# Transposing q and k by DMA instead of on TensorE, with the first batch's token stages put back whole

## The chip, the cores and the metric

The kernel runs on one core of a Trainium2 chip. The metric is device time in microseconds (us), the median of several runs. The engines are named as the profile names them: PE (TensorE, matrix products), PEld (its weight loads, which overlap PE), DVE (VectorE), ACT (ScalarE), POOL (GpSimd, which issues the loads), SP (SyncE, which issues the stores). Each engine works through its own queue in order.

## What is computed

Sliding-window attention with a position bias, followed by a token-and-channel mixer. The inputs are float32; the kernel works in bf16 and its output is float32.

```python
# q, k, v: (B, H, S, D) = (8, 8, 576, 64); window 128; slopes 2 ** -(h + 1)
scores = q @ k.T / sqrt(D) - slope_h * |i - j|     # only where 0 <= i - j < 128
attn   = softmax(scores) @ v
x = attn.transpose(0, 2, 1, 3).reshape(8, 576, 512)
h = relu(x^T @ w_tok1) @ w_tok2                    # over tokens: 576 -> 256 -> 576
u = x + h^T
out = u + relu(u @ w_ch1) @ w_ch2                  # over channels: 512 -> 1536 -> 512
```

## The kernel before, in words

**Groups.** Two heads of a batch make a group g; there are four groups per batch (NHP), 32 in all. For each group the kernel does:

- T (`att_T`, line 195): q and k of the group, tokens in the partitions, are transposed so that the head dimension is in the partitions. For the load, tokens are laid out as 96 partitions (RP) of six consecutive tokens (TPP) each, so a group needs 6 transposes of 96x128 for q and 6 for k. They go to one PSUM buffer; ACT copies q's half to `qT`, DVE copies k's half to `kT`, both putting the tokens in order. The argument `early` uses two smaller PSUM buffers and gives both copies to ACT.
- S, E, M (`att_S`, `att_E`, `att_M`), in two halves: scores on PE, exponential with bias on ACT, product with a mask on DVE.
- V (`att_V`, line 263): the weighted sum of v on PE, then a reciprocal and a product on DVE, which write `xb`. With `early` it works head by head.

**Loads.** `dma_qk(b, ...)` on POOL brings q and k of a batch, turned to bf16, into `qn` and `kn` (two each, by parity of the batch). `regroup` on DVE copies them to `qg` and `kg` (two each too), with the slices in the order that T reads. `dma_v` brings v into `vp`.

**Mixer.** For each batch: `tok1` (two, each five matmuls), `tok2` (five), `trans_u` (four, transposes of u), `ch1` (24, each four matmuls, whose relu on ACT writes R2), and the second channel product `ch2_items` (four or five chunks of 512 columns, each in three parts of four matmuls, then an add on DVE and a store on SP). The chunks of a batch run in the mixer of the next batch.

**Order.** The order in every queue is the order of the program text. `spread` (line 17) interleaves a mixer's items with attention work of the batches ahead: main items and side items have weights, and a side item is emitted when its share of the side weight is reached by the main items' share. In the mixer of batch b the side work is `att_step` for four groups, which transposes groups two ahead, scores one ahead, and does V of the current one. In the mixer of batch b the transposes are so those of batch b+1's last two groups and of batch b+2's first two. The regroup for batch b+3 stands at channel tiles 4 and 7 of 12 in mixer b (line 491).

**The start.** Lines 506 to 628 are written out by hand. Batch 0's groups are worked on as the loads arrive. Its token stages run in pairs of heads (`tok1_pair`, `tok2_pair`, with `trans_u` between them), mixed into the attention of batch 0, so that the channel products of batch 0 begin at once after. Half of these run alone (line 604), then all attention of batch 1 is spread over the other half and the first six items of batch 1's mixer (line 614). Then batch 2 is regrouped and the rest of mixer 1 runs with groups 8 and on beside it.

**PSUM.** `ps_at` has two buffers of two banks each, shared in turn by T, S and V (and `tok2_pair`); `ps_ma` has four of one bank, shared by all of the mixer.

Of the kernel before, what the change touches and what calls it, by code (L numbers as in the profile page):

```python
# [38 lines left out]
def kernel(  # L39
# [38 lines left out]
    pepool = ctx.enter_context(tc.tile_pool(name="pe", bufs=3))  # L78
# [12 lines left out]
    qg = [const.tile([P, TPP, H, D], bf16, name=f"qg{i}") for i in range(2)]  # L91
    kg = [const.tile([P, TPP, H, D], bf16, name=f"kg{i}") for i in range(2)]
    vp = [const.tile([P, H, NCH, D + 1], bf16, name=f"vp{i}") for i in range(2)]
    NR = 4
# [26 lines left out]
    def dma_v_tail(b):  # L121
        nc.gpsimd.dma_start(
            out=vp[b % 2][P - TAIL : P, :, NF, 0:D],
            in_=v[b, :, NF * P : S, :].rearrange("h s d -> s h d"),
        )

    def dma_v(b, c):
        nc.gpsimd.dma_start(  # L128
            out=vp[b % 2][:, :, c, 0:D],
            in_=v[b, :, c * P : (c + 1) * P, :].rearrange("h s d -> s h d"),  # L130
        )

    def dma_v_head(b, h):
        nc.gpsimd.dma_start(
            out=vp[b % 2][:, h, 0:NF, 0:D],
            in_=v[b, h, 0 : NF * P, :].rearrange("(c p) d -> p c d", p=P),
        )

    def regroup(b, h0, h1, which=(0, 1)):

        for n in which:
            raw, t = ((qn, qg), (kn, kg))[n]
            nc.vector.tensor_copy(  # L143
                out=t[b % 2][:RP, :, h0:h1, :],
                in_=raw[b % 2][:RP, h0:h1, :].rearrange("p h (j d) -> p j h d", j=TPP),
            )
# [48 lines left out]
    def att_T(g, early=False):  # L195
        b, hp = divmod(g, NHP)
        if early:
            tt = [ps_ma.tile([P, 1024], bf16, name="tT1", tag="ma") for _ in range(2)]
        else:
            t2 = ps_at.tile([P, 2, 1024], bf16, name="tT", tag="at")  # L200
            tt = [t2[:, n, :] for n in range(2)]
        for n, t_raw in ((0, qg), (1, kg)):
            for j in range(TPP):
                nc.tensor.transpose(  # L204
                    tt[n][:, j * RP : (j + 1) * RP],
                    t_raw[b % 2][:RP, j, 2 * hp : 2 * hp + 2, :].rearrange("p h d -> p (h d)"),
                    ident[:RP, :RP],
                )
        def nat(n):
            return tt[n][:, 0:S].rearrange("c (j p) -> c p j", j=TPP)  # L210
        def dst(a):
            return a[:, :].rearrange("c (p j) -> c p j", j=TPP)
        nc.scalar.copy(out=dst(qT[g % NR]), in_=nat(0))  # L213
        (nc.scalar.copy if early else nc.vector.tensor_copy)(out=dst(kT[g % NR]), in_=nat(1))  # L214

# [47 lines left out]
    def att_V(g, early=False):  # L263
# [5 lines left out]
        if early:  # L269
            ots = [ps_ma.tile([P, 512], f32, name="ot1", tag="ma") for _ in range(2)]  # L270
        else:
            ot = ps_at.tile([P, 2, 512], f32, name="ot", tag="at")
            ots = [ot[:, i, :] for i in range(2)]
        for i in range(2):
# [7 lines left out]
            for n, (qb, pb, col, kc) in enumerate(mms):  # L282
                nc.tensor.matmul(  # L283
                    ots[i][:, qb * (D + 1) : (qb + 1) * (D + 1)],
                    lhsT=pb[:, i, col : col + P], rhs=vb[:, h, kc, :],
# [3 lines left out]
        xs = xb[b][:, :, 2 * hp * D : (2 * hp + 2) * D].rearrange("p c (i d) -> p i c d", i=2)  # L289
        if early:  # L290
            for i in range(2):
                o3 = ots[i][:, 0 : NCH * (D + 1)].rearrange("p (c e) -> p c e", e=D + 1)
                nc.vector.reciprocal(out=rt[:, i, :, None], in_=o3[:, :, D : D + 1])
                nc.vector.tensor_tensor(  # L294
                    out=xs[:, i, :, :], in0=o3[:, :, 0:D],
                    in1=rt[:, i, :, None].broadcast_to([P, NCH, D]), op=ALU.mult,
                )
        else:
            o4 = ot[:, :, 0 : NCH * (D + 1)].rearrange("p i (c e) -> p i c e", e=D + 1)
            nc.vector.reciprocal(out=rt[:, :, :, None], in_=o4[:, :, :, D : D + 1])  # L300
            nc.vector.tensor_tensor(  # L301
                out=xs, in0=o4[:, :, :, 0:D],
                in1=rt[:, :, :, None].broadcast_to([P, 2, NCH, D]), op=ALU.mult,
            )
# [15 lines left out]
    def att_step(g):  # L320

        its = []
        if g + 2 < NG:
            its.append((0.6, lambda: att_T(g + 2)))
# [22 lines left out]
    def tok2(b, c):  # L347
        if c == 0:
            ubs[b] = upool.tile([P, NCH, DM], bf16, name="ub", tag="ub", bufs=3)
# [8 lines left out]
        )  # L358

    def tok1_pair(hp):  # L360

        t1 = ps_ma.tile([P, NDH, P], f32, name="t1p", tag="ma")
        for dh in range(NDH):
            for c in range(NCH):
                nc.tensor.matmul(
                    t1[:, dh, :], lhsT=W1[:, c, dh * P : (dh + 1) * P],
                    rhs=xb[0][:, c, hp * P : (hp + 1) * P],
                    start=(c == 0), stop=(c == NCH - 1),
                )
        r1t = rpool.tile([P, DM], bf16, name="r1t", tag="r1t", bufs=4)  # L370
        nc.scalar.activation(
            out=r1t[:, 0 : NDH * P], in_=t1[:, :, :].rearrange("p j x -> p (j x)"), func=ACT.Relu
        )
        r1s[hp] = r1t

    def tok2_pair(hp):
        if hp == 0:
# [286 lines left out]
```

## Time and profile before

| | |
|---|---|
| time, median of 3 runs | 328.44 us (328.26 to 331.09) |
| profiled execution, own time | 328.44 us |
| its span | 326.6 us |
| PE busy | 299.9 us (92%) |
| PEld busy | 194.2 us (59%) |
| ACT busy | 180.4 us (55%) |
| DVE busy | 178.6 us (55%) |
| POOL busy | 60.9 us (19%) |
| granted PE clock | 0.999 |
| the software DMA queue's packets (loads) | 55.3% of 16 engines' span |
| the hardware DMA queue's packets (stores) | 8.3% |

The span is the time from the first to the last instruction of one profiled execution. PE's busy time overstates how full PE is, because matmuls are pipelined and their ends are modelled: the distance between the starts of neighbouring matmuls is the better measure. Some groups of instructions that the change touches, with count, busy us and the mean of one:

| line | what | count | busy us | mean ns |
|---|---|---|---|---|
| L204 | PE, transposes of q and k | 384 | | 203 to 281 |
| L213 | ACT, copies to qT from PSUM | 32 | | about 640 |
| L214 | DVE, copies to kT from PSUM | 28 | 21.2 | 757 |
| L143 | DVE, regroup of a whole batch | 14 | 13.6 | 946 to 1070 |
| L245 | ACT, exponentials | 128 | 79.9 | 692 |
| L420 | ACT, relu after ch1 | 192 | 72.8 | 423 |
| L253 | DVE, product with the mask | 64 | 43.7 | 688 |
| L356 | DVE, u add of batches 1 to 7 | 35 | 22.9 | 683 |
| L388 | DVE, u add of batch 0, by pairs | 4 | 3.3 | 819 |

### The profile page before, as it was taken

Reading aid. Unit: us, or ns where it says so; the run is one execution under the profiler, and the core shown is the slowest. Engines: PE = TensorE matmul, PEld = TensorE weight load, DVE = VectorE, ACT = ScalarE, POOL = GpSimd, SP = SyncE. Lnnn points to the kernel's source line nnn. Section 1 sums busy time; section 2 is a strip of 40 time slices with the busy share of each in tenths; the row PEclk is TensorE's granted clock in tenths of the full one; section 3 lists DMA queues with packets and bytes.
Section 4 is the critical chain, followed back from the end, with each engine's and each line's share of the span. In section 5 each row is a group of like instructions: output and inputs, shape, how many; then the busy total and the mean of one; then the engine's idle time right before and its main releaser. Section 6 shows DMA issues by size and latency. Waiting matters only on the chain.

```text
span 326.6 us, 6808 instructions
## 1 busy us (share of the span) xinstructions
PE 299.9 (92%) x2876; PEld 194.2 (59%) x2876; DVE 178.6 (55%) x343; ACT 180.4 (55%) x379; POOL 60.9 (19%) x81
## 2 busy tenths in 40 slices
PE   2797978796999999998999999998999999999995
PEld 1475854443775567655775567755775567647742
DVE  4996246869554875358453775358433762343021
ACT  3973897171995328753795418743785139313800
POOL 8993151622015000410005000310000000000000
PEclk9999999999999999999999999999999999999999
DMA  6999999995879111991009110191001010011022
GB/s 87 157 165 203 200 167 154 217 159 115 134 102 147 37 67 38 157 89 66 34 0 100 39 66 34 11 95 65 35 2 32 34 69 30 2 64 64 2 64 97
DMA packets 59502, 27.76 MB, mean 85 GB/s; under 512 B 38672, under 2 KB 54864, under 8 KB 59472
## 3 DMA queue, kind: packets, MB, share of 16 engines
q0 software_dynamic: 54224, 17.90, 55.3%
q1 hardware_dynamic: 5248, 9.44, 8.3%
q8 instruction: 22, 0.36, 0.5%
q14 instruction: 8, 0.07, 0.1%
HBM read 35.78 MB, written 9.44 MB: 138 GB/s over the span
## 4 chain that ended last, share of the span: by engine, by line
PE 72%; DVE 16%; ACT 7%; DMA 2%; issue 1%; POOL 1%; POOLq 0%
PE ct L415 23%; PE ht L352 4%; PE sp L233 4%; PE tT L204 4%; ACT pe L245 4%; PE ot L283 4%; DVE pb L253 3%; DMA kn_87<-in_k_dram 2%; ACT R_104 L420 2%; DVE xb L301 2%; DVE ub L356 1%; DVE obt L455 1%; DVE xb L294 1%; DVE kT_100 L214 1%; PE ut L402 1%
## 5 line engine op out<-in xcount | busy, mean ns | idle before, releaser
L415 PE MATMUL ct<-UT,WC_107 128*128 128x288 bf16 x768 | 103.5, 286 | 2.7 <-DVE UT L407 1.6
L245 ACT ACTIVATE pe<-sp,biascol 128x512 bf16<-128x512 f32 x128 | 79.9, 692 | 19.4 <-PE sp L233 13.6
L420 ACT ACTIVATE R_104<-ct 128x288 bf16<-128x288 f32 x192 | 72.8, 423 | 32.1 <-PE ct L415 26.5
L415 PEld LDWEIGHTS <-WC_107 128*128 128x128 bf16 x768 | 72.4, 98 | 24.0 <-issue 5.0
L253 DVE TENSOR_TENSOR pb<-pe,masks 128x1024 bf16<-128x1024 bf16 x64 | 43.7, 688 | 50.8 <-ACT pe L245 50.8
L443 PEld LDWEIGHTS <-R_104 128*128 128x128 bf16 x432 | 40.3, 98 | 43.3
L283 PEld LDWEIGHTS <-pb 128*128 128x128 bf16 x576 | 22.9, 100 | 5.2 <-DVE pb L253 0.7
L356 DVE TENSOR_TENSOR ub<-ht,xb 128x512 bf16<-128x512 f32 x35 | 22.9, 683 | 3.8 <-PE ht L352 3.8
L128 POOL DMA_DIRECT2D vp_94<-in_v_dram x16 | 15.0, 945 | 49.6 <-PE ot L283 45.1
L301 DVE TENSOR_TENSOR xb<-ot,rt 128x640 bf16<-128x640 f32 x28 | 23.1, 824 | 1.0
L352 PE MATMUL ht<-r1t,W_106 128*128 128x512 bf16 x70 | 18.9, 379 | 0.0
L128 POOL DMA_DIRECT2D vp_93<-in_v_dram x12 | 10.5, 894 | 43.1 <-PE ot L283 35.4
L213 ACT COPY qT_95<-tT 128x576 bf16<-128x576 bf16 x7 | 4.5, 638 | 21.4 <-PE tT L204 21.2
L213 ACT COPY qT_98<-tT 128x576 bf16<-128x576 bf16 x7 | 4.5, 642 | 21.3 <-PE tT L204 21.3
L300 DVE RECIPROCAL rt<-ot 128x10 f32<-128x10 f32 x28 | 6.0, 215 | 12.2 <-PE ot L283 12.2
L204 PEld LDWEIGHTS <-qg_89 96*128 96x128 bf16 x96 | 6.1, 106 | 9.8 <-DVE qg_89 L143 8.1
L283 PE MATMUL ot<-vp_94,pb 128*128 128x65 bf16 x288 | 11.6, 194 | 0.2 <-DVE xb L301 0.2
L339 PEld LDWEIGHTS <-W_105 128*128 128x128 bf16 x70 | 6.4, 98 | 8.6 <-issue 1.5
L407 DVE COPY UT<-ut 128x576 bf16<-128x576 bf16 x28 | 11.1, 447 | 0.5 <-PE ut L402 0.5
L214 DVE COPY kT_101<-tT 128x576 bf16<-128x576 bf16 x7 | 5.3, 756 | 10.3 <-ACT qT_97 L213 10.3
L402 PE MATMUL ut<-ident,ub 128*128 128x128 bf16 x128 | 10.9, 219 | 0.0
L214 DVE COPY kT_99<-tT 128x576 bf16<-128x576 bf16 x7 | 5.3, 757 | 9.6 <-ACT qT_95 L213 9.6
(217 smaller groups left out, 394.9 us busy)
## 6 DMA issues: line engine op xcount, KB each, us to landing
out_dram<-obt SPq DMA_DIRECT2D x32, 256.0 KB, 2.0
qn_86<-in_q_dram POOLq DMA_DIRECT2D x4, 576.0 KB, 9.7
kn_88<-in_k_dram POOLq DMA_DIRECT2D x4, 576.0 KB, 11.5
vp_94<-in_v_dram POOLq DMA_DIRECT2D x16, 128.0 KB, 6.1
qn_85<-in_q_dram POOLq DMA_DIRECT2D x3, 576.0 KB, 9.3
kn_87<-in_k_dram POOLq DMA_DIRECT2D x3, 576.0 KB, 11.9
WC_107<-in_moe_w_ch_dram POOLq DMA_DIRECT2D x3, 512.0 KB, 9.0
WC_108<-in_moe_w_ch_dram POOLq DMA_DIRECT2D x1, 1536.0 KB, 22.9
```

Of the source, the lines that this page charges most:

```text
L128: nc.gpsimd.dma_start(out=vp[b % 2][:, :, c, 0:D], in_=v[b, :, c * P : (c + 1) * P, :].rearrange("h s d -> s h d"),)
L204: nc.tensor.transpose(tt[n][:, j * RP : (j + 1) * RP], t_raw[b % 2][:RP, j, 2 * hp : 2 * hp + 2, :].rearrange("p h d -> p (h d)"), ident[: ...
L245: nc.scalar.activation(out=pe[:, i, :], in_=sp[:, i, :], func=ACT.Exp, bias=biascol[:, h : h + 1], scale=scale,)
L253: nc.vector.tensor_tensor(out=pb[:, :, :], in0=pes.pop((g, half))[:, :, :], in1=masks[:, half, 2 * hp : 2 * hp + 2, :], op=ALU.mult,)
L283: nc.tensor.matmul(ots[i][:, qb * (D + 1) : (qb + 1) * (D + 1)], lhsT=pb[:, i, col : col + P], rhs=vb[:, h, kc, :], start=(n == 0), stop=( ...
L301: nc.vector.tensor_tensor(out=xs, in0=o4[:, :, :, 0:D], in1=rt[:, :, :, None].broadcast_to([P, 2, NCH, D]), op=ALU.mult,)
L352: nc.tensor.matmul(ht[:, :], lhsT=W2[:, j, c0(c) : c0(c) + P], rhs=r1s[b, j][:, :], start=(j == 0), stop=(j == NDH - 1),)
L356: nc.vector.tensor_tensor(out=ubs[b][:, c, :], in0=ht[:, :], in1=xb[b][:, c, :], op=ALU.add)
L402: nc.tensor.transpose(ut[:, main0 + c * P : main0 + (c + 1) * P], ubs[b][:, c, cb * P : (cb + 1) * P], ident[:, :],)
L415: nc.tensor.matmul(ct[:, :], lhsT=WC1[:, cb, ht_i * P : (ht_i + 1) * P], rhs=UT[:, cb, o : o + SH], start=(cb == 0), stop=(cb == NCB - 1),)
L420: nc.scalar.activation(out=R2[:, ht_i, o : o + SH], in_=ct[:, :], func=ACT.Relu)
L443: nc.tensor.matmul(o2[0][:, :], lhsT=R2[:, ht_i, col : col + P], rhs=WC2[:, ht_i, :], start=(ht_i == 0 and c != NF), stop=(ht_i == NHT - 1),)
```

## The change

For batches 2 to 7, `att_T` makes no PE transposes. Instead a new function, `dma_trans`, issues two DMA transposes per batch on SP: all of `qg` (96 partitions x 3072) into `tq`, all of `kg` into `tk`. The copies to `qT` and `kT` remain, one on ACT and one on DVE, now reading those tiles in SBUF. Batches 0 and 1 are transposed on PE as before. `qg` and `kg` become one tile each; `tq` and `tk` are two each. `dma_trans(b)` is called right after the regroup of batch b: in the mixer, after channel tile 7 of mixer b-3; by hand for batches 2 and 3.

The start is another one: batch 0's token stages are not done in pairs but after its attention, as for the other batches, mixed with regroup, transposes and scores of batch 1's first two groups; its UT copies move from ACT to DVE; the other two groups' scores are spread over the channel products of batch 0, and V of batch 1 over the first six items of mixer 1. After `dma_trans(2)` the next four items of mixer 1 (two `tok1`, two parts of a chunk) run without side work. v's tiles have another order of dimensions; some pools have a buffer less; loads are issued in another order.

```diff
-    pepool = ctx.enter_context(tc.tile_pool(name="pe", bufs=3))
+    pepool = ctx.enter_context(tc.tile_pool(name="pe", bufs=2))
...
-    qg = [const.tile([P, TPP, H, D], bf16, name=f"qg{i}") for i in range(2)]
-    kg = [const.tile([P, TPP, H, D], bf16, name=f"kg{i}") for i in range(2)]
-    vp = [const.tile([P, H, NCH, D + 1], bf16, name=f"vp{i}") for i in range(2)]
-    NR = 4
+    qg = const.tile([P, TPP, H, D], bf16, name="qg")
+    kg = const.tile([P, TPP, H, D], bf16, name="kg")
+    tq = [const.tile([P, TPP * NHP, RP], bf16, name=f"tq{i}") for i in range(2)]
+    tk = [const.tile([P, TPP * NHP, RP], bf16, name=f"tk{i}") for i in range(2)]
+    vp = [const.tile([P, NCH, H, D + 1], bf16, name=f"vp{i}") for i in range(2)]
+    NR = 3
...
+    def dma_trans(b):
+
+        for src, t in ((qg, tq), (kg, tk)):
+            nc.sync.dma_start_transpose(
+                out=t[b % 2][:, :, :], in_=src[:RP, :, :, :].rearrange("p j h d -> p (j h d)")
             )
...
     def att_T(g, early=False):
         b, hp = divmod(g, NHP)
+        if b < 2:
...
+            src = [t[:, 0:S].rearrange("c (j p) -> c p j", j=TPP) for t in tt]
         else:
+            src = [
+                t[b % 2][:, :, :].rearrange("c (j n) p -> c n p j", n=NHP)[:, hp, :, :]
+                for t in (tq, tk)
+            ]
+        dst = [t[g % NR][:, :].rearrange("c (p j) -> c p j", j=TPP) for t in (qT, kT)]
+        nc.scalar.copy(out=dst[0], in_=src[0])
+        (nc.scalar.copy if early else nc.vector.tensor_copy)(out=dst[1], in_=src[1])
...
-            its.append((0.6, lambda: att_T(g + 2)))
+            its.append((0.2, lambda: att_T(g + 2)))
...
-            ubs[b] = upool.tile([P, NCH, DM], bf16, name="ub", tag="ub", bufs=3)
+            ubs[b] = upool.tile([P, NCH, DM], bf16, name="ub", tag="ub", bufs=2)
...
-    def tok1_pair(hp):
...
-    def tok2_pair(hp):
...
-        (nc.vector.tensor_copy if b else nc.scalar.copy)(
-            out=UT[:, cb, o : o + S], in_=ut[:, :]
-        )
+        nc.vector.tensor_copy(out=UT[:, cb, o : o + S], in_=ut[:, :])
...
+                if ht_i == 7 and 0 < b < B - 3:
+                    its.append((0.0, lambda: dma_trans(b + 3)))
...
-        for h in range(4):
+        for h in range(H):
             dma_v_head(0, h)
...
-        for h in range(4, H):
-            dma_v_head(0, h)
+        dma_qk(1, 0, H)
...
         att_T(3, True)
-        att_V(0, True)
         build_masks(3)
...
+        att_SEM(2, 1)
+        att_V(0)
+        att_SEM(3, 0)
+        att_V(1)
+        att_SEM(3, 1)
+        att_V(2)
+        att_V(3)
...
+        order = t1 + [
+            lambda: regroup(1, 0, H), lambda: att_T(g), lambda: att_T(g + 1),
+            t2[0], t2[1], lambda: att_SEM(g, 0), t2[2], t2[3], lambda: att_SEM(g, 1), t2[4],
+            lambda: att_SEM(g + 1, 0), *ut, lambda: att_SEM(g + 1, 1),
+        ]
...
+        spread([(0.48, f) for f in c1], side)
+        spread(its1[:n1], [(0.6, lambda x=x: att_V(g + x)) for x in range(NHP)])
         regroup(2, 0, H)
+        dma_trans(2)
...
+        side.append((0.0, lambda: dma_trans(3)))
...
-        spread(its1[n1:], side)
+        for _, f in its1[n1 : n1 + NDH + 2]:
+            f()
+        spread(its1[n1 + NDH + 2 :], side)
```

## The prediction

> **What bounds the kernel now.** I read the page's busy times first, then the table of busy time by stage, then TensorE's (PE's) timeline in one steady mixer, then the fill, then the DMA issues.
>
> The page says PE is busy 92% of the span, but an average hides two regimes. The table by stage (columns: stretch, its length, busy us and count of PE, PEld, DVE, ACT, POOL, then clock, DMA share, GB/s) separates them:
>
> ```profile
> 0.00:32.20 32.20, 20.88 (x263) 15.30 (x264) 24.09 (x90) 19.62 (x33) 25.39 (x39) 1.00 1.24 152
> 32.20:61.40 29.20, 24.39 (x278) 17.25 (x278) 15.55 (x25) 20.69 (x44) 8.32 (x11) 1.00 1.92 180
> 61.40:98.50 37.10, 32.76 (x359) 22.00 (x359) 24.93 (x39) 24.61 (x52) 8.96 (x11) 1.00 1.11 138
> 98.50:135.70 37.20, 36.91 (x356) 23.52 (x354) 22.22 (x37) 21.39 (x47) 5.63 (x7) 1.00 0.60 86
> ...
> 172.30:210.00 37.70, 37.41 (x361) 23.95 (x359) 21.89 (x37) 21.41 (x46) 4.39 (x6) 1.00 0.36 52
> ```
>
> From 98.5 on PE lacks only 0.3 us of 37; DVE and ACT are busy under 60%. Before 61.4 it idles 16 us: the fill, where DVE, ACT and latencies set the end. In steady state, then, PE time saved is time saved. The PE timeline of the mixer of batch 4 shows the price of one transposed group (start, length, line, operation):
>
> ```profile
> 174.04 0.42 PE L204 MATMUL tT<-ident,qg_90 96*128 96x96 bf16 x6
> 174.30 0.42 PE L204 MATMUL tT<-ident,kg_92 96*128 96x96 bf16 x6
> 174.56 1.03 PE L443 MATMUL o_2632<-WC_108,R_104 128*128 128x512 bf16 x4
> ```
>
> Starts are what counts, since ends are modelled: from 174.04 to 174.56, 12 transposes hold PE for 0.52 us, 43 ns each.
>
> **Part 1: TensorE transposes of batches 2 to 7 go.** 6 batches x 4 groups x 0.52 us = 12.5 us of PE. They lie from 62 us to the end of batch 7's, four per mixer: two in the stretch of second channel products, one among the transposes of u, one in the first channel product. Where PE has no gap all of it is gained. In the last of these stretches ACT could take over: the 16.5 us from 193.0 to 209.5 hold 13.4 us of ACT, and from 202.3 to 209.5 ACT is busy without a gap. I discount half of that one group in five mixers: 5 x 0.26 = 1.3. Gain 11.2; bounds 9.4 (a whole group per mixer lost, and the 0.5 us of one more) and 14 (the second half of the scores also waited 0.2 to 0.3 us at 67.0, 88.4 and 94.9 for the PSUM buffer that a transposed group held, which for these batches is no longer taken).
>
> The Trainium skill speaks against the change here: "VectorE: DVE Perf Modes", section "The three transpose paths", gives 390 ns for a 128x128 transpose on TensorE and 1309 ns by DMA, and its rules prefer TensorE where PSUM will do. The 43 ns pitch disagrees with the first figure; by the second, one DMA here (18 such blocks) would be an estimated 23.6 us if nothing overlapped, which is the second rival below.
>
> **Part 2: the copies stay.** Each group keeps its copy of qT on ACT (638 ns) and kT on DVE (757 ns), now from SBUF with a stride of 768 B instead of 192 B. No row has this read; regroup reads in runs at 96x3072 in 950 ns, faster per element. Between 0.4 and 1.5 us each on engines that are not the bound: taken as unchanged.
>
> **Part 3: DMA transposes arrive.** Twelve, each 96x3072 bf16 = 576 KB, on SP's queue, which carries only outputs (332 ns to issue one). SP's in-order queue now waits for the regroup before it can issue, and outputs stand behind it; three output buffers and 2.6 us or more between outputs cover some microseconds. How long one takes (L) no row shows. From the nearest rows:
>
> ```profile
> out_dram<-obt SPq DMA_DIRECT2D x32, 256.0 KB, 2.0
> qn_86<-in_q_dram POOLq DMA_DIRECT2D x4, 576.0 KB, 9.7
> kn_88<-in_k_dram POOLq DMA_DIRECT2D x4, 576.0 KB, 11.5
> ```
>
> At least 2.0 us (an output on the same queue, less than half the bytes), at most 11.9 (the page's slowest load of the same bytes, software queue, reading float32). I take 4.5 us, the output row scaled by bytes (2.0 x 576/256), since queue and packet path are nearest. By the skill's "DMA: Bandwidth & Descriptors", "Latency and other measured facts" (261 GB/s for DMA transposes) with that page's fixed 2 us, L would be an estimated 4.3 us; no run here shows it yet.
>
> Who waits? For batches 4 to 7 the issue stands at the eighth of twelve channel tiles of a mixer and the first use near the middle of the next mixer, over 20 us later: hidden up to L = 10 in series. For batch 2 it is not. Before, the first tok1 of batch 1 starts at 61.4 and its regroups end at 62.2 and 63.4, that is 0.8 and 2.0 us later. After, the transposes start then. The code runs two tok1 (2.2 us) and two parts (1.7) first, then the spread places one part (0.86) and one tok2 (0.43) before group 8's scores: cover of 5.2 us. Scores are ready at: k transposed, plus kT's copy 0.85. In series: 0.8 + 9.0 + 0.85 = 10.6, a stall of 5.4; side by side: 2.0 + 4.5 + 0.85 = 7.4, a stall of 2.2. I take 4. Ends: L = 2 in series, 4.8 + 0.85, 0.4 us; L = 11.9 side by side 9.6, in series 20. ACT and DVE queue up behind these two copies (relu, ub), so PE cannot run far past them. For batch 3 the scores come about 10 us after the issue: 0, but 4 at L = 11.9 side by side and 15 in series. One qg and one kg also make the next regroup wait until these were read; a mixer later, free.
>
> **Part 4: the fill goes back to whole-batch stages.** Now group 3's xb is stored at 28.1 and the first ct starts at 31.3, since token stages ran pair by pair under the scores. After, masks and exponentials still set the pace up to xb (DVE is 9.2 us busy from 10 to 20); without the four ub adds (3.3 us) but with each product behind its own exponential, I leave it at 28.1. Then DVE's queue must run, before ct: swap 0.6, regroup of batch 1 1.9, two kT 1.5, five ub adds of 0.68, three products of 0.69, four UT copies of 0.45 = 11.3 us. With about 1 us of gaps ct starts at 40.4, 9 us late, but four of eight score halves of batch 1 are done. ACT then has 24 relu x 0.42 + 5 exponential pairs x 1.2 + 2 qT x 0.64 = 17.4 us against 14.4 of PE: about 57.5. Then six parts of 0.86 and four value groups of 0.57 on PE, 7.5 us, and the last xb 0.4: 65.4, where now it is 61.3. Loss 4; bounds 1 (ACT's tail overlaps the parts) and 8 (gaps as the 5 us that this stretch shows now).
>
> **Smaller edits.** Fewer buffers (qT/kT 4 to 3, exponentials 3 to 2, ub 3 to 2): each is reused at least a step after its last reader. The order of vp and the spread weight 0.2 touch no bound: nothing. q and k of batch 1 loaded ahead of the channel weights: those are now issued at 17.1 and land in 11 us or less, and ct comes 9 us later: covered, else 2 us.
>
> **Sum.** The profiled run's own time is 328.44, span 326.6 and 1.84 around it; it is also the median. 328.4 - 11.2 + 4 + 4 = 325.2, rounded to 325.
>
> **Rivals.**
> - *Cover suffices.* Transposes of 2 to 3 us in series: 0.4 to 2 us of stall, fill at its lower half: 328.4 - 12 + 2.5 + 1 = 320. For it: no large DMA elsewhere on SP's queue. Against: value loads of batch 2 and q and k of batch 4 are issued at 60.4 to 66, with the DMA engines 90% busy or more up to 73.
> - *The DMA becomes the wait (slower).* Place: group 8's scores, then batch 3's. It decides when the two stalls exceed 7.2 + 3.3 us: with 2L - 3.55 for batch 2 and 2L - 9.15 for batch 3 in series that is L = 5.8, side by side (L - 2.35 and L - 8.2) L = 10.5. At 11.9 side by side: 328.4 - 11.2 + 4 + 9.6 + 4 = 335; in series, with 20 and 15, 356, and every mixer would begin to wait. For it: the 9.7 to 11.9 us rows. Against: those read float32 from HBM.
> - *The fill costs more, about 8 to 10* with the stall of 4: 329 to 331. For: 5 us of PE gaps in that stretch now.
> - *It does not do what it says:* if the transposes were split in element-sized pieces, the second rival at its far end; part of its chance.
>
> **Numbers.** No-change shows within about 1%, 325.2 to 331.7 (the three runs span 328.3 to 331.1). Forecast 0.42 (its own range 321 to 328; 0.25 faster, 0.17 same), cover suffices 0.20 (faster), DMA wait 0.28 (slower), heavier fill 0.10 (0.04 same, 0.06 slower). Faster 0.45, same 0.21, slower 0.34. The range, 319 to 340, leaves out the DMA wait's far end (0.13) and the best of the second case (0.06).
>
> **What would show it.** Right: L204 x96 instead of x384; mixers from 98.5 on about 2 us shorter each; a wait of ACT's qT or DVE's kT copy on the DMA of tq or tk once, near 70 us; first ct near 40. Wrong: landing times of tq and tk of 9 us or more with waits in every batch; copies from SBUF well over 1 us; ct pitch growing as much as the transposes saved; a gap at the fill outside 1 to 8 us.

## The result, and the profile after

The changed kernel takes 343.85 us (median of 4 runs, 342.79 to 345.94) where the kernel before took 328.35 beside it: ratio 1.0459 with a 95% interval of 1.0384 to 1.0535, so it is slower by 4.6%. Forecast was 325, with a range of 319 to 340. The profiled run's own time is 344.43, its span 342.7. Medians here and below are of all runs, while ratios and intervals leave out the runs that are more than 1.5% above the fastest of the same kernel.

First the table of busy time by stage of the changed kernel, in the columns of the one before. Its stretches are the kernel's own: to just before the first `ct` (which is at 42.1), to the first `tok1` of batch 1 (65.6), to the end of the wait described below (85.3), to the first chunk product of mixer 2 (122.5), and the rest.

| stage ends at | before | after | its length, after less before |
|---|---|---|---|
| first `tok1` of batch 1 | 61.4 | 65.6 | +4.2 |
| first chunk product of mixer 2 | 98.3 | 122.5 | +20.0 |
| end of the span | 326.6 | 342.7 | -8.1 |

The second row is read from PE's timeline, before and then after:

```profile
98.27 0.39 PE L437 MATMUL o_1575<-ident,UT 128*128 128x128 bf16 x4
```

```profile
122.48 0.39 PE L405 MATMUL o_1427<-ident,UT 128*128 128x128 bf16 x4
```

The busy times of the stretches after:

```profile
0.00:41.00 41.00, 24.70 (x234) 15.09 (x235) 30.40 (x92) 21.76 (x35) 27.07 (x41) 0.98 1.23 162
41.00:65.60 24.60, 23.38 (x250) 16.54 (x248) 11.43 (x21) 15.26 (x36) 6.63 (x8) 0.96 2.02 162
65.60:85.30 19.70, 5.34 (x26) 2.26 (x27) 3.45 (x5) 3.41 (x4) 5.55 (x6) 0.71 1.37 174
85.30:122.50 37.20, 30.34 (x259) 18.45 (x260) 21.24 (x37) 24.19 (x47) 3.53 (x5) 0.83 0.65 96
122.50:342.70 220.20, 212.86 (x1768) 130.38 (x1765) 110.23 (x189) 122.69 (x251) 19.03 (x22) 1.00 0.51 78
```

Read the PE column against the length of the stretch. The last stretch is as full as before (212.9 of 220.2 us, before 222.1 of 228.3), and shorter. The loss is in the third and fourth: of 56.9 us PE works in 35.7, and the granted clock is 0.71 and 0.83. The chain of waits between 70 and 86 says which wait ends last (start, length, what):

```profile
70.52 0.70 DVE obt L423
71.23 0.07 SPq L153
71.30 0.05 issue
71.34 13.20 DMA tk_93<-kg
84.55 0.02 issue
84.57 0.66 DVE kT_102 L227
85.23 0.05 issue
85.28 1.03 PE sp L246 x10
```

One DMA, the transpose of k of batch 2, lies on the path with 13.2 us. PE's timeline gives the gap from PE's side: 14.36 us before the scores of group 8, then three gaps that end on work which had queued behind batch 3's copies.

```profile
85.28 1.03 PE L246 MATMUL sp<-qT_99,kT_102 64*128 64x256 bf16 x10 [14.36 <-DVE kT_102 L227]
...
109.14 0.65 PE L383 MATMUL ct<-UT,WC_107 128*128 128x288 bf16 x4 [1.35 <-ACT R_104 L388]
110.59 0.65 PE L383 MATMUL ct<-UT,WC_107 128*128 128x288 bf16 x4 [0.80 <-ACT R_104 L388]
...
117.48 0.39 PE L246 MATMUL sp<-qT_97,kT_100 64*128 64x256 bf16 x6 [2.25 <-DVE xb L300]
```

The releasers ACT R and DVE xb are not the cause there. Both engines had been held in their own queues by a copy that waited for a transposed tile of batch 3 (ACT 2.39 us for `tq_92`, DVE 7.89 us for `tk_94`), and the relu and the product stood behind it, as ACT's and DVE's timelines show:

```profile
107.62 1.16 ACT L226 COPY qT_97<-tq_92 128x576 bf16<-128x576 bf16 x1 [2.39 <-DMA tq_92<-qg]
```

```profile
113.65 0.71 DVE L227 COPY kT_100<-tk_94 128x576 bf16<-128x576 bf16 x1 [7.89 <-DMA tk_94<-kg]
```

The transposes among the DMA issues of the page (at the end of each line the median us from issue to landing; a row holds three batches) and SP's queue (start, length of the issue):

```profile
tq_91<-qg SPq DMA_TRANSPOSE x3, 10.0
tk_93<-kg SPq DMA_TRANSPOSE x3, 13.2
tq_92<-qg SPq DMA_TRANSPOSE x3, 8.8
tk_94<-kg SPq DMA_TRANSPOSE x3, 10.9
```

```profile
66.42 4.88 SPq L153 DMA_TRANSPOSE tq_91<-qg  x1
71.34 8.46 SPq L153 DMA_TRANSPOSE tk_93<-kg  x1
79.85 15.39 SPq L426 DMA_DIRECT2D out_dram<-obt  x2
98.81 3.92 SPq L153 DMA_TRANSPOSE tq_92<-qg  x1
102.77 6.92 SPq L153 DMA_TRANSPOSE tk_94<-kg  x1
```

Batches 2 to 5 land in about 9 to 17 us each. Batches 6 and 7 land in 4.6 to 5.1: no load of q and k is left, and those of v begin at 192.3 and 228.1, about 1 and 2 us before the last one of the pair lands. The issue alone holds SP for up to 8.5 us, and in order, so the second transpose of a pair starts that much later.

### The profile page after: what moved, and what is told of

The parts are those of the page before. It is cut to its first block, busy times and chain, and to the rows that moved or that the text cites. A ratio compares the mean times of both kernels' runs of the same rounds, so it can differ in the third digit from the quotient of the medians.

```text
span 342.7 us, 6139 instructions
## 1 busy us (share of the span) xinstructions
PE 296.6 (87%) x2528; PEld 182.7 (53%) x2528; DVE 176.7 (52%) x340; ACT 187.3 (55%) x373; POOL 61.8 (18%) x81
## 4 chain that ended last, share of the span: by engine, by line
PE 69%; DVE 10%; ACT 10%; DMA 8%; issue 3%; POOL 0%; SPq 0%; POOLq 0%
PE ct L383 21%; ACT pe L258 5%; PE ht L355 5%; PE ot L292 4%; DMA tk_93<-kg 4%; PE sp L246 4%; DMA tk_94<-kg 3%; ACT R_104 L388 3%; DVE pb L266 2%; DVE xb L300 2%; DVE obt L423 1%; DVE ub L359 1%; PE ut L372 1%; DVE UT L377 1%; PE o_1014 L411 1%
## 5 line engine op out<-in xcount | busy, mean ns | idle before, releaser
L258 ACT ACTIVATE pe<-sp,biascol 128x512 bf16<-128x512 f32 x128 | 80.1, 692 | 61.1 <-PE sp L246 60.5
L383 PE MATMUL ct<-UT,WC_107 128*128 128x288 bf16 x768 | 105.8, 292 | 5.7 <-ACT R_104 L388 4.1
L383 PEld LDWEIGHTS <-WC_107 128*128 128x128 bf16 x768 | 74.3, 99 | 30.2 <-issue 9.2
L411 PEld LDWEIGHTS <-R_104 128*128 128x128 bf16 x432 | 40.7, 99 | 45.2 <-issue 1.8
L359 DVE TENSOR_TENSOR ub<-ht,xb 128x512 bf16<-128x512 f32 x40 | 26.1, 682 | 5.6 <-PE ht L355 5.6
L300 DVE TENSOR_TENSOR xb<-ot,rt 128x640 bf16<-128x640 f32 x32 | 26.4, 824 | 1.1
L355 PE MATMUL ht<-r1t,W_106 128*128 128x512 bf16 x80 | 22.1, 392 | 0.0
L246 PE MATMUL sp<-qT_99,kT_102 64*128 64x256 bf16 (+2 forms) x100 | 7.7, 280 | 15.1 <-DVE kT_102 L227 14.4
L130 POOL DMA_DIRECT2D vp_95<-in_v_dram x12 | 10.8, 914 | 41.0 <-PE ot L292 32.7
L292 PE MATMUL ot<-vp_95,pb 128*128 128x65 bf16 x288 | 13.6, 209 | 1.8 <-DVE xb L300 1.7
L342 PEld LDWEIGHTS <-W_105 128*128 128x128 bf16 x80 | 8.2, 104 | 12.7 <-issue 4.8
L246 PEld LDWEIGHTS <-kT_102 64*128 64x128 bf16 x100 | 4.2, 101 | 20.0 <-DVE kT_102 L227 14.8
L377 DVE COPY UT<-ut 128x576 bf16<-128x576 bf16 x32 | 12.7, 448 | 0.8 <-PE ut L372 0.5
L118 POOL DMA_DIRECT2D qn_86<-in_q_dram x4 | 3.4, 838 | 53.5 <-DVE qg L145 52.7
L355 PEld LDWEIGHTS <-W_106 128*128 128x128 bf16 x80 | 7.5, 100 | 9.0 <-issue 1.3
L292 PE MATMUL ot<-vp_96,pb 128*128 128x65 bf16 x288 | 11.4, 193 | 0.0
## 6 DMA issues: line engine op xcount, KB each, us to landing
vp_96<-in_v_dram POOLq DMA_DIRECT2D x16, 128.0 KB, 11.2
```

The source lines that it names most:

```text
L130: nc.gpsimd.dma_start(out=vp[b % 2][:, c, :, 0:D], in_=v[b, :, c * P : (c + 1) * P, :].rearrange("h s d -> s h d"),)
L246: nc.tensor.matmul(sp[:, hh, i * 256 + x0 : i * 256 + x1], lhsT=kt[r, k0 : k0 + P], rhs=qt[r, q0 : q0 + x1 - x0], start=True, stop=True,)
L258: nc.scalar.activation(out=pe[:, i, :], in_=sp[:, i, :], func=ACT.Exp, bias=biascol[:, h : h + 1], scale=scale,)
L292: nc.tensor.matmul(ot[:, i, qb * (D + 1) : (qb + 1) * (D + 1)], lhsT=pb[:, i, col : col + P], rhs=vb[:, kc, h, :], start=(n == 0), stop=(n ...
L300: nc.vector.tensor_tensor(out=xb[b][:, :, 2 * hp * D : (2 * hp + 2) * D].rearrange("p c (i d) -> p i c d", i=2), in0=o4[:, :, :, 0:D], in1 ...
L355: nc.tensor.matmul(ht[:, :], lhsT=W2[:, j, c0(c) : c0(c) + P], rhs=r1s[b, j][:, :], start=(j == 0), stop=(j == NDH - 1),)
```

## The experiments

Theory: the price of the transposes, once they run beside the loads on POOL's queue, is what was wrong; the other terms hold. Rivals: the new start costs more than 4 us, the strided read of the copies holds ACT, the half clock after a gap is the loss, or the outputs behind the transposes on SP are late. All kernels compute the whole result. The kernels were run in four groups, each beside the kernel before on the same chip.

| kernel | time, us | ratio to before, 95% |
|---|---|---|
| e1: all transposes on PE, new start | 338.22 | 1.030 [1.024, 1.035] |
| e11: the same, spread weight 0.6 | 332.19 | 1.009 [1.005, 1.012] |
| e3: loads later in the program text | 338.17 | 1.029 [1.025, 1.034] |
| e6: PE kept busy in the gap | 344.78 | 1.044 [1.038, 1.049] |
| e7: batch 2 transposed earlier | 330.10 | 1.001 [0.997, 1.005] |
| e12: loads held until batch 2 is copied | 326.59 | 0.992 [0.989, 0.995] |
| e13: earlier, and loads held | 323.38 | 0.984 [0.979, 0.988] |
| e14: e13, shorter read stride | 322.51 | 0.984 [0.976, 0.993] |
| e15: e13's transposes on the old start | 329.75 | 1.003 [1.000, 1.005] |
| e17: e15 with contiguous reads, strided writes | 338.44 | 1.032 [1.025, 1.038] |
| e18: e15 with both copies on DVE | 329.94 | 1.002 [0.998, 1.006] |
| e19: e15, batch 5's loads held too | 324.05 | 0.984 [0.977, 0.990] |
| e20: e13, batch 5's loads behind batch 3's `tk` | 327.34 | 0.995 [0.992, 0.999] |
| e22: e19, batch 4's loads held too | 331.41 | 0.997 [0.991, 1.004] |

**The new start alone (e1, e11).** The changed kernel without its DMA transposes: all batches go through TensorE, `qg` and `kg` are two each.

```diff
-        if b < 2:
+        if b < B:
...
-                if ht_i == 7 and 0 < b < B - 3:
-                    its.append((0.0, lambda: dma_trans(b + 3)))
...
-        dma_trans(2)
...
-        side.append((0.0, lambda: dma_trans(3)))
```

> The changed kernel with all 32 groups transposed on TensorE (qg and kg two each again, no tq and tk, no DMA transposes); its new start is kept. Theory A (the DMA transposes of batches 2 and 3 come too late; the start costs 4 us): the time is that of before plus the start, 328.4 + 4 = 332.5, no gap near 70 us and a granted clock of 1.0 throughout. Rival C (the new start and its order cost most of the 16 us): 340 or more.

It came out at 338.22, above that. Two causes had been mixed. The first `tok1` of batch 1 starts at 66.1, 4.7 later than before, as the start's term has it. But the change's weight of 0.2 puts a group's transposes close ahead of the next scores, and with transposes on PE they share the two PSUM buffers: the second half of the scores waits for a buffer, in the steady mixers too. One of four such waits in mixers 2 and 3 of e1:

```profile
107.70 0.40 PE L232 MATMUL sp<-qT,kT 64*128 64x256 bf16 x6 [0.33 <-DVE kT L213]
```

e11 puts the weight of before back, in both places, and changes nothing else:

```diff
-            its.append((0.2, lambda: att_T(g + 2)))
+            its.append((0.6, lambda: att_T(g + 2)))
...
-        side = [(0.2, lambda: att_T(2 * NHP)), (0.2, lambda: att_T(2 * NHP + 1))]
+        side = [(0.6, lambda: att_T(2 * NHP)), (0.6, lambda: att_T(2 * NHP + 1))]
```

> All 32 groups on TensorE in the new order (as e1), with the side weight of a group's transposes back at 0.6 in the two places where the change made it 0.2. In e1 (338) the second half of each group's scores waited 0.3 to 1.2 us for the PSUM buffer that the transposes just ahead of it held. Theory A: the new start alone costs 4 to 5 us (its first tok1 of batch 1 comes 4.7 us late in e1) and the rest of e1's loss is this distance between transposes and scores: 333. Rival: the start costs the whole 9 to 10 us later on too: 338 again.

332.19 beside 329.6: the start, together with the smaller edits that e11 keeps, costs 2.6 us by the medians (1.7 to 4.0 by the interval), where 4 was taken, and the weight 6.0 us. In mixers 2 and 3 of e11 no scores wait, and the two take 73.7 us (102.02 to 175.73), as before (73.8, from 98.27 to 172.09), where e1 takes 76.4 (104.42 to 180.83). In the changed kernel itself the later groups hold no PSUM buffer for their transposes, so the weight's price does not fall due there.

**The loads beside the transposes (e3, e12).** e3 moves the loads of v of batch 3 and of q and k of batches 4 and 5 behind later steps of the text.

```diff
-        if hp == NHP - 1 and b + 2 < B:
+        if hp == NHP - 1 and b + 2 < B and b != 1:
...
-            dma_qk(4, 0, H)
...
+        side.append((0.0, lambda: ([dma_v(3, c) for c in range(NF)], dma_v_tail(3), dma_qk(4, 0, H))))
...
+            if g == 2 * NHP + 2:
+                side.append((0.0, lambda: dma_qk(5, 0, H)))
```

> The changed kernel with the loads that run beside the transposes moved behind them: v of batch 3 and q, k of batch 4 after group 8's scores, q, k of batch 5 after group 12's copies. Theory A1 (contention with the loads makes them late: 11 to 17 us here against 5 for batch 6, which has no loads beside it): tq of batch 2 lands about 5 us after its issue and tk 8 after it, group 8's scores start near 75 instead of 85.3, the gap is 4 us instead of 14.4; time 328 to 333. Rival A2 (a transpose of this size takes this long by itself when its tile is first used): landing stays above 10 us and the time stays at 340 to 345.

Half of the edit did nothing: POOL had nothing else queued, so v of batch 3 still went out at 63.7 and q and k of batch 4 at 68.9, as soon as their buffers were free. Batch 2's transposes still landed in 12.1 and 14.9 us. Only q and k of batch 5 moved, from 99.1 to 113.0; they now stand behind those of batch 6, which went out at 108.9. Batch 3's transposes then had no loads beside them and their waits went: the first chunk product of mixer 2 starts at 115.2 instead of 122.5, and the time falls by 5.7 us (338.17 for 343.85). That is batch 3's part of the loss.

e12 holds POOL with a real dependency: a copy of one column that reads `kT` of group 8 goes ahead of the loads of v of batch 3 and q and k of batch 4, into a tile that nothing reads. Batch 5's loads stand as in e3.

```diff
...
+        side.append((0.0, lambda: (
+            nc.gpsimd.tensor_copy(out=gate[:, :], in_=kT[(2 * NHP) % NR][:, 0:1]),
+            [dma_v(3, c) for c in range(NF)], dma_v_tail(3), dma_qk(4, 0, H),
+        )))
...
```

> The changed kernel with the loads of v of batch 3 and q, k of batch 4 really held back: a one-column copy on POOL that needs group 8's kT stands before them in POOL's queue (in e3 they were only moved in the text, and started at the same time as before). q, k of batch 5 late as in e3. Theory A1 (contention with loads): tq and tk of batch 2 land 5 us after their issue, each issued in about 3 us; group 8's scores start at 75 to 76, a gap of 4 to 5 us; no clock loss after it; 325 to 328. Rival A2 (slow by itself): issue of 5 and 8 us and the gap of 14 stay; 338 as e3.

The same two transposes at the same place, with nothing beside them, now from SP's queue and PE's timeline of e12:

```profile
66.17 3.05 SPq L154 DMA_TRANSPOSE tq<-qg  x1
69.27 3.07 SPq L154 DMA_TRANSPOSE tk<-kg  x1
```

```profile
74.93 1.03 PE L247 MATMUL sp<-qT,kT 64*128 64x256 bf16 x10 [4.25 <-DVE kT L228]
```

They land in 5.1 and 4.9 us, and the gap is 4.25 us instead of 14.36. The time is 326.59 instead of 343.85, with the start, the copies and the saving on PE unchanged. The DMA engines' share by queue while the transposes are under way tells why; first the changed kernel from 66 to 85, then e12 from 66 to 75 (share of 16 engines at the end of each line, packets and MB ahead of it; packets of two queues can be under way on an engine at once, so the shares can add to more than 100%):

```profile
DMA packets 11137, 3.29 MB, mean 173 GB/s; under 512 B 9425, under 2 KB 10978, under 8 KB 11137
...
q0 software_dynamic: 6274, 1.78, 95.3%
q1 hardware_dynamic: 4863, 1.51, 45.2%
```

```profile
DMA packets 4872, 1.53 MB, mean 169 GB/s; under 512 B 4696, under 2 KB 4708, under 8 KB 4872
...
q1 hardware_dynamic: 4859, 1.52, 79.8%
q0 software_dynamic: 13, 0.01, 0.7%
```

The hardware queue (the transposes and one output) has nearly the same 1.5 MB in both, and the time of its packets is nearly the same too: 45.2% of 19 us is 8.6, 79.8% of 9 us is 7.2. But they are through in 9 us alone and in 19 beside 1.78 MB of loads, whose packets take 95.3% of the engines' time: the transposes are late because they share the engines with the loads. The mean rates, 173 and 169 GB/s, do not show a limit, since in e12 the engines stand idle for a part of the window. What in the engines runs out, bytes or packets, was not separated, nor the loads of v from those of q and k.

**The clock (e6).** In the gap the granted clock of the changed kernel falls: 0.88, 0.50, 0.50, 0.50, 0.91 in the five windows of 5 us from 70 to 95, with PE idle from 70.9 to 85.3. The Trainium skill says this too ("TensorE: Matmul & The Clock Gate", Part 1: half rate after an idle window of about 3.4 us), and by it the work after the gap should be worth speeding up. e6 adds 60 matmuls, whose result is not used, in the gap.

```diff
+        for _ in range(3):
+            wm = ps_ma.tile([P, 512], f32, name="wm", tag="ma")
+            for n in range(20):
+                nc.tensor.matmul(
+                    wm[:, :], lhsT=WC2[:, 0, 0:P], rhs=WC2[:, 1, :], start=(n == 0), stop=(n == 19)
+                )
+            nc.vector.tensor_copy(out=wmo[:, :], in_=wm[:, 0:1])
```

> The changed kernel with 60 unused matmuls of 512 columns (12.8 us) put in TensorE's queue into the gap before group 8's scores, and three copies of one column each. Theory: part of the loss is not the gap but the lower granted clock after it (0.50 from 75 to 90 us): the work from 85.3 to 90.8 then takes 3 us instead of 5.9, so the time falls by about 3 us, to 341, with the gap's length unchanged. Rival: the clock's fall costs nothing, as the engines behind wait anyway: 344, or 346 if the unused work delays the scores.

The time did not fall by the medians (344.78 for 343.85), but the runs scatter from 341.86 to 347.11, so the times alone don't rule out a gain of 3 us. The traces say more. The clock from 64 to 100 rose from 0.76 to 0.95, and from group 8's scores to the first channel product it took 9.6 us (84.75 to 94.37) where the changed kernel took 10.6 (85.28 to 95.89). Then batch 3's copies waited for the same transposes (ACT 3.56 us for `tq`, DVE 9.38 for `tk`, where the changed kernel shows 2.39 and 7.89); `tk` landed at 113.6 in both, and the scores behind it went on at 117.4 and 117.5. What the clock gave, 1 us, the next late DMA took. So the half clock shows no cost of its own in this kernel. What it would cost without batch 3's wait was not tried.

**An earlier issue (e7, e13, e14).** e7 regroups and transposes batch 2 while the channel products of batch 0 still run, and batch 3 where batch 2 was.

```diff
+        side.append((0.0, lambda: (regroup(2, 0, H), dma_trans(2))))
         side += score_items(g + 3)
...
-        regroup(2, 0, H)
-        dma_trans(2)
+        regroup(3, 0, H)
+        dma_trans(3)
...
```

> The changed kernel with the regroup and the DMA transposes of batch 2 moved ahead, behind the last TensorE transpose of batch 1 (about 12 us earlier), and those of batch 3 to where those of batch 2 stood. Nothing else. Theory A (what is lost is the missing lead of batches 2 and 3 and the clock after it): no gap before group 8's scores, clock 1.0, and the time is before + 4 for the start - 9 to 12 for the TensorE transposes = 320 to 324. Rival B (the transposes cost more in steady state than they save, through ACT's copies, 1.19 us instead of 0.64, and the DMA queues): 330 or more.

330.10, with ten runs from 328.08 to 336.65; the profile is of one of 328.91. The transposes went out at 54.7 and 62.2 and took 15.0 and 13.9 us, now beside the loads of batch 3. A new wait came with the single `qg` and `kg`: batch 3's regroup may not write them until the late transposes have read them, and DVE stands still for that, with all that is queued behind it (DVE's timeline of e7):

```profile
69.77 0.96 DVE L145 COPY qg<-qn 96x3072 bf16<-96x3072 bf16 x1 [3.37 <-DMA tq<-qg]
76.19 0.96 DVE L145 COPY kg<-kn 96x3072 bf16<-96x3072 bf16 x1 [5.45 <-DMA tk<-kg]
```

e13 takes the earlier issue for batch 2 only, and holds the loads of batch 3 back until `tk` has landed. Batch 5's loads are moved as in e3.

```diff
+        side.append((0.0, lambda: (
+            regroup(2, 0, H), dma_trans(2),
+            nc.gpsimd.tensor_copy(out=gate[:, :], in_=tk[0][:, 0, 0:1]), dma_qk(3, 0, H),
+        )))
...
-            order.append(lambda: dma_qk(3, 0, H))
...
-        regroup(2, 0, H)
-        dma_trans(2)
```

> The changed kernel with regroup and transposes of batch 2 right after the last TensorE transposes of batch 1, and q, k of batch 3 loaded only when tk of batch 2 has landed (POOL waits for it); batch 3's transposes where the change has them, with q, k of batch 5 loaded later. Theory A: no gap at group 8 or 12, granted clock near 1.0 after 60 us; 320 to 323 (328.4 + 4 for the start - 9 to 12). In e7 a regroup of batch 3 waited for the slow transposes of batch 2 in DVE's queue, which cost the 6.5 us that remained there. Rival B (steady cost of ACT's copies and the queues): 327 or more without any gap.

323.38, below the kernel before and well below the changed one. The gap at group 8's scores is 0.91 us, and batch 3's wait is down to gaps of 1.88 and 0.81, the first of which stands here:

```profile
70.03 0.61 PE L247 MATMUL sp<-qT,kT 64*128 64x256 bf16 x10 [0.91 <-DVE kT L228]
...
92.04 0.65 PE L384 MATMUL ct<-UT,WC 128*128 128x288 bf16 x4 [1.88 <-ACT R L389]
```

e14 is e13 with `qg` and `kg` laid out group first, so that the copies read with a stride of 192 B instead of 768.

```diff
...
-                t[b % 2][:, :, :].rearrange("c (j n) p -> c n p j", n=NHP)[:, hp, :, :]
+                t[b % 2][:, :, :].rearrange("c (n j) p -> c n p j", n=NHP)[:, hp, :, :]
```

> As e13, with qg and kg ordered by group first (group, token step, heads), so that the copies to qT and kT read tq and tk with a stride of 192 B, as they read PSUM before, instead of 768 B; the regroup writes another order. If ACT's 1.19 us (0.64 from PSUM) comes from the stride, the copy falls to about 0.65 and the time by 0 to 2 us against e13, since ACT is near its limit only in the first channel product. If it comes from reading SBUF at any stride, the copy stays at 1.2 and the time is e13's.

322.51, not to be told from e13. ACT's copy takes 1204 ns, as in the changed kernel (1192 to 1211 by buffer), so the stride of 768 B is not what makes it slower than the 638 ns of the copy from PSUM.

**The old start with DMA transposes (e15, e17, e18, e19).** If the start costs 2.6 us, the transposes of e13 on the start of before should do better than e13. e15 is the kernel before with e13's edits, the transposes by DMA, and the change's weight of 0.2 and smaller pools for `ub`.

> The kernel before with its own start kept (batch 0's token stages by pairs) and only the DMA transposes added for batches 2 to 7, timed as in e13: batch 2's right behind the last TensorE transposes of batch 1 and ahead of the load of q, k of batch 3, which waits for tk; q, k of batch 5 late. Theory A, with parts that add up: e13's 323.4 minus the 3 to 4 us that the new start costs (e11: 332.2 against 329.6 and the 66.1 against 61.4 of its first tok1): 319 to 321. Rival: the two parts overlap (DMA engines busier in the start, transposes late again): 323 to 327 with a gap at group 8 or 12.

It took 329.75. Group 8 is in time (a gap of 0.78), but batch 3's pair, issued at 79.3 and 85.8, took 17.0 and 12.6 us beside the loads of v of batch 3 and q and k of batches 4 and 5, which on this start went out by 80.1. The wait moved to batch 3:

```profile
97.87 3.04 PE L432 MATMUL ct<-UT,WC 128*128 128x288 bf16 x12 [9.14 <-ACT R L437]
```

e17, with the group-first layout of e14, reads the transposed tiles in runs and writes with a stride of 12 B instead; e18 gives the copy of qT to DVE as well.

```diff
...
-            dst = [t[g % NR][:, :].rearrange("c (p j) -> c p j", j=TPP) for t in (qT, kT)]
+            dst = [t[g % NR][:, :].rearrange("c (p j) -> c j p", j=TPP) for t in (qT, kT)]
```

> As e15, with qg and kg ordered by group first and the copies to qT and kT reading 576 elements in a row and writing with a stride of 12 B, in place of a strided read and a contiguous write. If ACT's 1.19 us comes from strided reads of SBUF (at 768 B as at 192 B, e14), it falls to about 0.65; if ACT reads bf16 from SBUF at that pace in any order, it stays at 1.2. Time: 0 to 2 us under e15 in the first case, e15's in the second.

```diff
-            nc.scalar.copy(out=dst[0], in_=src[0])
+            nc.vector.tensor_copy(out=dst[0], in_=src[0])
```

> As e15, with both copies of a DMA-transposed group on DVE (0.65 us each) and none on ACT (1.19 us). 24 x 1.19 = 29 us less on ACT, 24 x 0.65 = 16 us more on DVE. If ACT's longer copy is what keeps the steady gain at 8 us instead of 9.4 for the 18 groups after mixer 1 (ACT busy without a gap in the first channel product), the time falls by 1 to 3 us against e15; if DVE's queue then delays PSUM's release, it is the same or up to 3 us more.

e17 is slower (338.44): with the strided write ACT's 24 copies take 2143 ns each and DVE's 1159, where e15 shows 1210 and 667. The strided write is the dear side, on both engines.

e18 moves 24 copies of 1.2 us off ACT to 0.65 us each on DVE, and the time stays (329.94 for 329.75). DVE then waits 10.8 us for `tq` where ACT had waited 9.8. That wait could hide a gain in the time, but the steady mixers have no such wait: mixers 2 and 3 take 70.3 us in e15 (108.52 to 178.81) and 70.0 in e18 (106.99 to 176.98). So ACT's longer copies cost there only 0.3 us in two mixers more than the same copies on DVE.

e19 adds a hold to e15: q and k of batch 5 wait until batch 3's `tk` has landed.

```diff
-        side.append((0.0, lambda: dma_trans(3)))
+        side.append((0.0, lambda: (
+            dma_trans(3), nc.gpsimd.tensor_copy(out=gate[:, :], in_=tk[1][:, 0, 0:1]), dma_qk(5, 0, H),
+        )))
...
-            if g == 2 * NHP + 2:
-                side.append((0.0, lambda: dma_qk(5, 0, H)))
```

> As e15, with q, k of batch 5 held back in POOL's queue until tk of batch 3 has landed (in e15 they were issued at 78.0 and 80.1, just as batch 3's transposes were issued at 79.3, and those took 17.0 and 12.6 us; TensorE then stood for 9.1 us behind ACT's copy of group 12). Contention theory: batch 3's transposes land in 5 to 9 us, the 9.1 us go, 320 to 323. Rival (v of batch 3 and q, k of batch 4, issued at 67 to 73, are what they meet): part of the wait stays, 325 to 329.

324.05, between the two. Batch 3's `tk` is issued in 4.22 us instead of 10.51, ACT waits 2.98 us for `tq` instead of 9.78, and the gap of 9.14 us becomes one of 2.34. This confirms the cause of e15's time. The held loads now meet batch 4's transposes, which land in 17.9 and 17.5 us instead of 8.9 and 15.5, under cover. That the old start should then beat the new one by 2.6 us is not borne out: e19 and e13 can't be told apart.

**How far holding loads goes (e20, e22).** e20 is e13 with the hold of e19. e22 is e19 with q and k of batch 4 behind the same hold, and batch 4's regroup and transposes three to four channel tiles later.

> As e13 (the changed kernel's start), with the same hold on q, k of batch 5. In e13 these were late in any case, so nothing should move: 322 to 324. If it is faster by 2 us or more, e13 still lost time to loads beside batch 3's or 4's transposes.

> As e19, with q, k of batch 4 also loaded only after tk of batch 3 has landed, and batch 4's regroup and transposes moved from channel tiles 4 and 7 to 10 and 11 of mixer 1. If the loads of batch 4 are what batch 3's transposes meet in e19, these fall to about 5 us and the time to 319 to 321; if not, it equals e19, or is up to 3 us slower where batch 4's regroup waits for its later load.

e20 is 4 us slower than e13. In e13 q and k of batch 5 stand behind those of batch 6 and go out at 98.64 and 99.41; with the hold they go out sooner, at 93.58 and 94.82, as soon as batch 3's `tk` has landed. So more loads meet batch 4's first transpose, and its issue takes 8.11 us instead of 2.78. The transposes had cover, but the outputs behind them in SP's queue had not. SP's queue of e20, and the DVE instruction that needs an output buffer back:

```profile
94.53 8.11 SPq L154 DMA_TRANSPOSE tq<-qg  x1
102.75 10.95 SPq L154 DMA_TRANSPOSE tk<-kg  x1
113.80 0.58 SPq L421 DMA_DIRECT2D out_dram<-obt  x1
```

```profile
122.00 0.69 DVE L424 TENSOR_TENSOR obt<-o,ub 128x512 f32<-128x512 f32 x1 [1.50 <-DMA out_dram<-obt]
```

In e13 the second issue took 8.88 us from 97.65 and the store went out at 106.62, 7 us earlier, and no DVE instruction waits for a store. PE shows a gap of 1.08 for it in e20; the span is 2.8 longer, of which the rest was not followed. e22's ten times scatter from 325.8 to 337.0, too far for a verdict. Its profile is of the longest run and says nothing of the shorter ones; what decides between them is open.

## Why the prediction was wrong, point by point

- **Part 1, the saving on PE (taken 11.2): right for the three quarters of it that can be read.** From mixer 2 on, 18 of the 24 groups are left, whose share of 11.2 is 8.4; that stretch is 8.1 us shorter. Four mixers from mixer 2 on take 147.6 us before (98.27 to 245.91), 36.9 each, and 140.3 after (122.48 to 262.82), 35.1 each: 1.8 less, which is 4 x 0.52 less the 0.26 that was discounted. The other six groups lie in the stretch of the waits, where no run shows their part alone.
- **Part 4, the start (taken 4, bounds 1 to 8): right.** The last `xb` was put at 65.4 and `tok1` starts at 65.58, before at 61.36. The first `ct` came at 42.1, not 40.4, and what follows up to `xb` was shorter by as much. Part of so close a hit is luck: two errors cancel, and in other profiles with this start the first `tok1` comes at 63.7 (e6), 64.9 (e3) and 65.3 (e12). Alone (e11) the start costs 2.6.
- **Part 3, L: the step that failed.** L was taken as 4.5 us from an output row of the same queue, with little beside it. Alone that is nearly right: 4.9 and 5.1 us in e12, and the stall "I take 4" is 4.25. But the place was not a quiet one. The prediction itself says that value loads and q and k of batch 4 go out there, with the DMA engines 90% busy up to 73, and uses it only against the rival that cover suffices, not in L. With that, k landed 13.2 us after an issue that itself came 4.9 late, and the gap was 14.36. The estimate of 4.3 us from the Trainium skill's "DMA: Bandwidth & Descriptors" ("Latency and other measured facts") was nearly right for quiet engines too, and the row does not say how busy the engines were. The prediction's 23.6 us, for blocks that do not overlap, is more than any landing in these runs (20 at most), and is not in the rival to which it points, whose far end is 11.9.
- **"For batch 3: 0".** It follows from the same L. Its waits cost 5.7 us by e3's time, 7.2 by its first chunk product of mixer 2 (0.7 of that was there at the first `tok1`).
- **The sum.** 326.59 is what the kernel takes once the loads are kept away from batches 2 and 3 (e12), where the forecast was 325 (own range 321 to 328). The 17.3 us from there to 343.85 are what the loads beside the transposes cost. In the prediction's own terms, the stall of 4 for batch 2 was 14.4 and the 0 for batch 3 was 5.7 to 7.2, which makes 16 to 18 of the 18.7 us between 325.2 and 343.85.
- **The rival that the DMA becomes the wait** named the place and the order (group 8, then batch 3) and priced it 335 at L = 11.9 side by side, 356 in series. The chip did something between: SP's issue of one transpose ends before the next begins, but their landings overlap. The row for its far end, the page's slowest load, was the nearest of all rows, since the transposes share the engines with just those loads. "Those read float32 from HBM" was no argument against it. "Every mixer would begin to wait" did not happen: batch 4's 10.0 and 16.6 us were covered by more than 20.
- **Part 2, the copies "unchanged": half wrong, almost without effect.** ACT's went from 638 to 1200 ns, DVE's from 757 to 650. e18 takes ACT's away and gains 0.3 us in two mixers.
- **"The spread weight 0.2 touch no bound: nothing"** holds for this kernel, since the transposes that would block the PSUM buffer are gone. With them it is 6 us (e1 against e11).
- **The outputs behind the transposes on SP** were named with a cover of three buffers. In the changed kernel that cover held: no instruction waits for a store there. It breaks in e20.

## What to carry to other kernels

A DMA's duration belongs to its moment: look up which loads the other queues have under way at that time, and if the engines are full, price it by the rows of those loads at least, not by a row from a quiet stretch. Moving a load down in the program text delays nothing if its queue is idle; a dependency does, and the held load then meets the next transfer, so follow it one stage further. Where a queue's issue is slow, price what stands behind it in that queue, outputs and buffer reuse included.

## What the runs showed of the hardware

- An SBUF-to-SBUF transpose of 96x3072 bf16 (576 KB) lands in 4.6 to 5.4 us where no load is under way, and holds SP's queue for 2.8 to 3.8 us; in the midst of loads on the software queue it takes 8 to 20 us and holds SP for up to 12 (11.76 in e19).
- The granted clock is 0.50 in the windows after a gap's first 4 us, and stays there for about 5 us of work: 0.50 from 85 to 90 and 0.91 from 90 to 95, where work began at 85.3. A gap of 4.25 us was enough too: 0.51 from 75 to 80 in e12. Between gaps of 1 to 2 us in e13 it fell to 0.78 at the lowest, in 90 to 95.
- ACT copies 128x576 bf16 from SBUF in 1.20 us where it takes 0.64 from PSUM, for read strides of 768 and 192 B alike; with a strided write of 12 B it takes 2.14. DVE takes 0.65 and 1.16 for the two.
